# A gate on GpSimd's queue for batch 1's loads, in a fused FNet mixing and RWKV channel mix

## The chip, the cores and the metric

The kernel runs on one core of a Trainium2 chip. The core has five engines with a queue of instructions each: TensorE (PE, with its weight loads shown apart as PEld), VectorE (DVE), ScalarE (ACT), GpSimd (POOL) and SyncE (SP). They run independently of each other and meet at semaphores. Sixteen DMA engines move data between the main memory (DRAM) and the core's memory; here POOL issues all loads of x and of the weights, and SP nearly all stores of the output. The metric is the device time of one execution, in microseconds (us); lower is better.

## The reference

For each of 8 batches of x (3072 x 256), a two-dimensional Fourier transform of which the real part is kept, and then a channel mix with a shift by one row:

```python
X = np.fft.fft(x, axis=1)
X = np.fft.fft(X, axis=2)
x = X.real                                   # (8, 3072, 256)
x_prev = np.concatenate([zeros, x[:, :-1, :]], axis=1)
xk = mu_k * x + (1.0 - mu_k) * x_prev
xr = mu_r * x + (1.0 - mu_r) * x_prev
k = np.maximum(xk @ w_k, 0.0)                # 256 -> 1024
v = k * k @ w_v                              # 1024 -> 256
r = 1.0 / (1.0 + np.exp(-(xr @ w_r)))        # 256 -> 256
out = r * v
```

## The kernel before, in words

**One batch** passes through two halves. The transform uses the symmetry of a real input. Two copies of x are loaded for a batch, `xp` (rows in order) and `xm` (rows mirrored, fetched by a gather with a list of row numbers), each in two parts h = 0 and 1 (`load_xh`, L151). `fold` (L158) adds the two copies on DVE (L168 the bulk, L170 one column), `butterfly` (L173) splits the sum into an even and an odd part. Stage A (`a_sum`, `a_item`, `a_half`, L510 to 577) multiplies them with small tables on PE and leaves `a`; stage D (`d_units`, L579, with `d_evac` and `turned`, which repairs one column) goes on to `g_all`; stage C (`c_sums`, L624, or `c_pairs`, L651) gives the transform `y`. The results of PE lie in PSUM banks, and ACT or DVE copy them to the core's memory (L501 on DVE, L503 on ACT). `diff` and `mix` form xk and xr from y on DVE.

The channel mix runs over 48 chunks of 512 rows (8 batches, 2 mirrored halves m, 3 pieces). A chunk takes four steps of the main loop at the end of the kernel, some 2.2 us each. In a step PE multiplies with `w_k` (`k_products`, L738), ACT takes the positive part (L748), DVE or ACT squares it (L758, L756), PE multiplies an earlier chunk's squares with `w_v` (L779, L791 in the first chunks), and DVE multiplies the result with r and SP stores it (L801, L809). `r_item` (L760) gives r of a chunk: PE at L765 with `wr`, ACT at L770.

**The order of the work** is written out by hand. `at(step, f, ...)` and `event(step, ...)` put the transform of later batches between the chunks of earlier ones; `pin_order` at the end fixes the order on every engine to the order in which the code recorded it. Nothing else holds an instruction back than its semaphores: a load that is recorded at a late step starts as soon as POOL has done what stands ahead of it and the buffer is free. There are three buffers each for `xp` and `xm`, used in turn, and a load waits for the fold that read its buffer last.

**The start** is a stretch of its own. The tables are computed on the chip. Batch 0's x is loaded in six pieces (L242 to L249), and then `loads` (L441) puts on POOL's queue: the row numbers, the two halves of `w_k`, `w_v`, batch 1's first part (three loads: xp, one short xm, one long xm), the two halves of `w_r` for m = 0, and batch 1's second part (two loads). `loads_2`, recorded at step 4, follows with more row numbers and the weights for m = 1, and batch 2's loads after that. Meanwhile PE, DVE and ACT carry batch 0 through stages A, D and C in an order that mixes their pieces (L830 to L936). A few matmuls on zeros, `keep_busy` (L203), stand between them. The pieces around the change are, in the order of the code: two small pieces of stage D, one large piece with its first half evacuated by ACT (L854), one more piece of stage D (`w`), the first `c_sums` (slots 0 to 4), `turned(2, 4)` evacuated by DVE (L864), and the second half of the large piece evacuated by DVE (L865). Then come the first mixed columns (L869 on ACT, L874 on DVE), the `c_sums` of slots 5 to 8 and 9 to 16, and the first chunk's products.

Batch 1's first fold is on DVE at step 4 (`at(4, fold, 1, 0)`), its second at step 11; the first `r_item` is on PE at step 5. For later batches the loads of batch b + 3 are recorded 12 and 14 steps into batch b.

Of the kernel before, what the change touches and what calls it, by code (L numbers as in the profile page):

```python
# [11 lines left out]
INT32 = mybir.dt.int32  # L12
# [8 lines left out]
def _v(ap, extra_offset, free_dims):  # L21
    new_ap = [list(ap.ap[0])] + [[s, c] for (s, c) in free_dims]
    return dataclasses.replace(ap, offset=ap.offset + extra_offset, ap=new_ap)
# [16 lines left out]
def kernel(  # L40
# [20 lines left out]
    const = ctx.enter_context(tc.tile_pool(name="const", bufs=1))  # L61
# [44 lines left out]
    V = nc.vector  # L106
# [11 lines left out]
    def x_tiles(b, h):  # L118
        xp_t[b, h] = xp_sb[(2 * b + h - 1) % 3] if b or h else xp_00
        xm_t[b, h] = xm_sb[(2 * b + h) % 3]  # L120
# [6 lines left out]
    def load_p(b, h):  # L127
        r, n = 9 * h, 9 - h
        if b > 1:
            for g in range(2):  # L130
                src = dataclasses.replace(x[b, 32 * g + r:32 * g + r + 1, :],
                                          ap=[[64 * D, N1], [D, n], [1, D]])
                nc.gpsimd.dma_start(out=xp_t[b, h][64 * g:64 * g + N1, 0:n], in_=src)  # L133
            return
        src = dataclasses.replace(x[b, r:r + 1, :], ap=[[32 * D, 96], [D, n], [1, D]])
        nc.gpsimd.dma_start(out=xp_t[b, h][0:96, 0:n], in_=src)

    def gather(dst, src, idx):
        nc.gpsimd.indirect_dma_start(dst, None, src, bass.IndirectOffsetOnAxis(ap=idx, axis=0))  # L139

    def load_m(b, h, o, n, idx):
        gather(xm_t[b, h][0:parts(b), XM0 + o:XM0 + o + 256 * n],
               x.rearrange("b (s r) d -> (b s) (r d)", r=n), idx)

    def load_m0(b):
        if b == 0:
            gather(xm_00[:, 1:257], x.rearrange("b s d -> (b s) d"), idx_0[:, 0:1])
        else:
            load_m(b, 0, 2048, 1, (idx_g0 if b > 1 else idx_0)[:, b:b + 1])

    def load_xh(b, h):  # L151
        x_tiles(b, h)
        load_p(b, h)
        if h == 0:
            load_m0(b)
        load_m(b, h, 0, 8, (idx_g8 if b > 1 else idx_8)[:, b, h:h + 1])
# [74 lines left out]
    iota = nc.gpsimd.iota  # L231
# [191 lines left out]
    def rows():  # L423
        for a in range(2):
            for half in range(2):
                iota(_v(row_i[64 * half:64 * half + 64], a, [(3 - 2 * a, 2)]), pattern=[[0, 2]],
                     base=256 * a + half * (1 - 2 * a), channel_multiplier=2 - 4 * a)
        iota(row_i[0:1, 2:3], pattern=[[0, 1]], base=0, channel_multiplier=0)
        iota(_v(row_i[0:1], 1, [(2, 2)]), pattern=[[0, 2]], base=128, channel_multiplier=0)
# [11 lines left out]
    def loads():  # L441
        rows()
        for a in range(2):
            gather(wk_sb[0][a], moe_w_k, row_i[:, a:a + 1])
        nc.gpsimd.dma_start(out=wv_sb, in_=moe_w_v.rearrange("(fc p) v -> p fc v", p=128))
        load_xh(1, 0)
        for a in range(2):
            gather(wr_sb[0][a], moe_w_r, row_i[:, a:a + 1])
        load_xh(1, 1)

    def loads_2():
# [47 lines left out]
    def evac(out_ap, in_ap, eng):  # L499
        if eng == "V":  # L500
            V.tensor_copy(out=out_ap, in_=in_ap)  # L501
        else:
            nc.scalar.activation(out=out_ap, in_=in_ap, func=AF.Copy)  # L503
# [86 lines left out]
    def d_evac(ps, u0, n, bank, eng):  # L590
        evac(_v(g_all, 256 * u0, [(64, 2), (128, 2 * n), (1, 64)]),
             _v(ps, 0, [(bank, 2), (64, 2 * n), (1, 64)]), eng)
# [13 lines left out]
    def turned(u0, u1, ps=None, eng="A"):  # L606
        ps = ps_w() if ps is None else ps
        f128 = _v(g_all, 256 * u0 + 128, [(256, u1 - u0)])
        nc.tensor.matmul(out=ps[:, 0:u1 - u0], lhsT=turn, rhs=f128, start=True, stop=True)  # L609
        evac(f128, ps[:, 0:u1 - u0], eng)  # L610
# [222 lines left out]
    half_tables(mu_ps)  # L833
    V.tensor_copy(out=muf_t, in_=mu_ps[:, 0:6])
    loads()
    fold(0, 1, 0, 4)
    a_sum(0, 1, 0, "A")
# [25 lines left out]
    c_sums((first[:, 0:512], first[:, 512:1024]), 0, 5, 1)  # L863
    turned(2, 4, small[1][:, 256:258], "V")  # L864
    d_evac(fill[:, 256:1024], 4, 2, 512, "V")  # L865
    x_t[0, 0, 0] = mix_pool.tile([P, 2, 1536], FP16, name="x00")
    for a in range(2):
        t = x_t["t", a] = mix_pool.tile([P, 24, 64], FP16, name=f"t{a}")
# [28 lines left out]
    def at(step, f, *args):  # L897
        work.setdefault((step, "x" if f in (a_item, a_sum, d_item, d_small, c_item, c_tiles, turned, minus_0, r_item) else "w"),
                        []).append((f, args))
# [5 lines left out]
    def event(step, *items):  # L905
        work.setdefault((step, "e"), []).extend((f[0], f[1:]) for f in items)
        if len(items) > 2 and items[0][0] is not a_slots_0:
            early_v.add(step + 1)
# [102 lines left out]
    for b in range(B):  # L1011
        s0 = 24 * b

        for n, st0 in enumerate((2, 4, 6, 8) if b > 1 else ()):
            at(s0 + st0, mix, b, n // 2, 1, n % 2)
        if b and b + 3 < B:
            for h in range(2):
                at(s0 + 12 + 2 * h, load_xh, b + 3, h)
        t = b + 2
        if t < B:  # L1020
            if b:
                for n, st0 in enumerate((9, 10, 12, 14)):
                    at(s0 + st0, butterfly if n % 2 else fold, t, n // 2)
                for n, st0 in enumerate((27, 29, 31, 33)):
                    at(s0 + st0, d_item, t, n)
                at(s0 + 34, turned, 0, 13)
            c = [(c_pairs, t, 8 * n, (8, 8, 8, 4)[n], EV[n]) for n in range(4)]
            if t + 1 < B:
                event(s0 + ES[0], c[0], c[1], (a_half, t + 1, 0, 0, EV[4]))
                event(s0 + ES[1], c[2], c[3], (a_half, t + 1, 0, 1, EV[5]))  # L1030
                event(s0 + ES[2], (a_slots_0, t + 1), (a_half, t + 1, 1, 0, EV[6]), (a_half, t + 1, 1, 1, EV[7]))
            else:
                event(s0 + ES[0], *c[:2])
                event(s0 + ES[1], *c[2:])
        t = b + 1
        if b and t < B:
            at(s0 + 16, halves, t, 0, 15)
            at(s0 + 18, halves, t, 15, 27)
            for a in range(2):
                at(s0 + 19 + a, diff, t, 0, 26, (a,))  # L1040
                at(s0 + 21 + a, mix, t, 0, 0, a)
            at(s0 + 24, mix, t, 1, 0, 0)
            at(s0 + 25, mix, t, 1, 0, 1)
# [59 lines left out]
```

## Time and profile before

| | us |
|---|---|
| median of three runs | 441.21 (441.04 to 443.92) |
| the profiled execution, whole | 442.6 |
| its span, first to last instruction | 440.8 |
| PE busy in the span | 427.9 (97%) |
| DVE busy | 362.2 (82%) |
| ACT busy | 321.7 (73%) |
| POOL busy | 57.6 (13%) |

The profile is of one execution on the chip. The span lies inside the profiled time; 1.8 us are around it. All positions below are in microseconds from the start of the span. A row of the timeline gives the start, the duration, the engine, the line, the operation, what it writes and reads, the shape, how many instructions are merged, and in brackets how long the engine was idle before and what ended the wait; "remote" and "another core or an unknown queue" mean that the profile could not tell who ended it. A matmul's end is modelled. For a load, the row on POOL is only the issue; the data arrive later.

### The profile page before, as it was taken

What the parts mean: (1) busy time and instruction counts of PE and PEld (TensorE: products, weight loads), DVE (VectorE), ACT (ScalarE), POOL (GpSimd) and SP (SyncE); (2) the same over time, 40 slices, a digit from 0 to 9 for tenths busy, and PEclk for the clock granted to TensorE, in tenths of its full rate; (3) what the DMA queues carried; (4) which work ended last, traced back from release to release, by engine and by line L of the source; (5) the groups of instructions that cost most, each with busy time, mean ns of one, the idle gap of its engine ahead of it and who ended that gap; (6) DMA issues with size and microseconds to landing.
All of it is one profiled execution on the core that took longest, in us unless ns stands there. A gap on an engine that the chain in (4) does not pass through costs nothing.

```text
span 440.8 us, 9300 instructions
## 1 busy us (share of the span) xinstructions
PE 427.9 (97%) x3853; PEld 301.0 (68%) x3853; DVE 362.2 (82%) x554; ACT 321.7 (73%) x374; POOL 57.6 (13%) x83
## 2 busy tenths in 40 slices
PE   8699999999999999999999999999999999999995
PEld 3466766777777757677577776777776776766764
DVE  8589989998898968988699888989889857997553
ACT  7479898787877768687686778777777877666661
POOL 7862423004200120002100010000000000000000
PEclk9879999999999999999999999999999999999999
DMA  7999569239623493326732372322223223233334
GB/s 137 153 209 186 96 126 177 59 73 164 137 50 73 90 173 73 73 56 120 158 73 49 71 149 51 74 67 54 59 64 72 64 58 73 49 71 72 73 72 96
DMA packets 34990, 41.81 MB, mean 95 GB/s; under 512 B 4098, under 2 KB 31076, under 8 KB 34948
## 3 DMA queue, kind: packets, MB, share of 16 engines
q1 hardware_dynamic: 27524, 25.05, 24.2%
q0 software_dynamic: 7264, 16.04, 22.4%
q8 instruction: 30, 0.49, 0.5%
q10 hardware_dynamic: 160, 0.13, 0.1%
q14 instruction: 12, 0.10, 0.1%
HBM read 32.08 MB, written 25.17 MB: 130 GB/s over the span
## 4 chain that ended last, share of the span: by engine, by line
PE 94%; DVE 1%; DMA 1%; POOL 1%; issue 1%; another core or an unknown queue 0%; ACT 0%; POOLq 0%
PE psW L738 38%; PE psV L779 36%; PE psW L765 10%; PE psV L791 3%; PE psW L586 2%; PE psW L546 1%; PE psW L659 1%; DMA xm<-in_x_dram,idx 1%; PE psW L627 1%; POOL xm L139 1%; DVE pq L501 1%; PE psW L203 0%; PE psV L564 0%; PE psW L564 0%
## 5 line engine op out<-in xcount | busy, mean ns | idle before, releaser
L748 ACT ACTIVATE rl<-psW 128x1024 f16<-128x1024 f32 x192 | 195.6, 1025 | 91.4 <-PE psW L738 87.6
L738 PE MATMUL psW<-x,wk 128*128 128x512 f16 (+1 forms) x776 | 197.0, 380 | 0.8 <-DVE pq L501 0.7
L779 PE MATMUL psV<-wv_sb,k 128*128 128x256 f16 x1424 | 184.4, 273 | 0.2
L779 PEld LDWEIGHTS <-k 128*128 128x128 f16 x1424 | 136.9, 98 | 36.4 <-issue 0.7
L758 DVE TENSOR_TENSOR k<-rl 128x2048 f16<-128x2048 f16 (+1 forms) x101 | 116.3, 1152 | 32.9 <-ACT rl L748 32.5
L738 PEld LDWEIGHTS <-wk 128*128 128x128 f16 x776 | 75.6, 99 | 54.6 <-issue 2.2
L801 DVE SCALAR_TENSOR_TENSOR o<-psV,r 128x512 f32<-128x512 f32 (+1 forms) x97 | 65.8, 681 | 15.2 <-PE psV L779 13.5
L703 DVE TENSOR_TENSOR x<-y,t 128x1536 f16<-128x1536 f16 (+2 forms) x72 | 61.6, 861 | 2.1
L765 PE MATMUL psW<-wr,x 128*128 128x256 f16 x384 | 49.8, 273 | 0.0
L770 ACT ACTIVATE r<-psW 128x1024 f16<-128x1024 f32 x48 | 48.9, 1018 | 0.8 <-PE psW L765 0.8
L765 PEld LDWEIGHTS <-x 128*128 128x128 f16 x384 | 37.5, 98 | 14.3 <-issue 0.2
L133 POOL DMA_DIRECT2D xp<-in_x_dram x24 | 13.0, 546 | 187.5 <-DVE p L170 187.2
L503 ACT ACTIVATE a<-psW 128x832 f16<-128x832 f32 x31 | 26.1, 863 | 3.9 <-PE psW L546 1.4
L503 ACT ACTIVATE g_all<-psW 128x1024 f16<-128x1024 f32 (+5 forms) x36 | 25.3, 703 | 0.9 <-PE psW L609 0.6
L139 POOL DMA_INDIRECT xm<-in_x_dram,idx_g x18 | 23.6, 1311 | 5.7 <-issue 5.7
L168 DVE TENSOR_TENSOR p<-xp,xm 112x2304 f16<-112x2304 f16 (+5 forms) x19 | 21.0, 1105 | 0.8 <-DMA xm<-in_x_dram,idx 0.8
L692 DVE TENSOR_SCALAR t<-d,muf_t 128x1536 f16<-128x1536 f16 (+2 forms) x40 | 20.7, 527 | 0.0
L692 DVE TENSOR_SCALAR t<-d,mu_m 128x1536 f16<-128x1536 f16 x32 | 19.7, 614 | 0.0
L586 PEld LDWEIGHTS <-a 128*128 128x128 f16 x208 | 14.8, 102 | 6.7 <-issue 0.6
L503 ACT ACTIVATE pq<-psW 128x1024 f16<-128x1024 f32 (+1 forms) x18 | 15.2, 880 | 4.6 <-PE psW L659 4.6
L501 DVE CAST pq<-psW 128x1024 f16<-128x1024 f32 x6 | 7.3, 1225 | 13.0 <-PE psV L779 8.0
L179 DVE TENSOR_TENSOR eo<-p 112x1152 f16<-112x1152 f16 (+3 forms) x28 | 18.0, 683 | 0.0
(136 smaller groups left out, 215.8 us busy)
## 6 DMA issues: line engine op xcount, KB each, us to landing
out_dram<-o SPq DMA_DIRECT2D x190, 128.0 KB, 2.4
xp<-in_x_dram POOLq DMA_DIRECT2D x12, 216.0 KB
xp<-in_x_dram POOLq DMA_DIRECT2D x12, 192.0 KB
xp<-in_x_dram POOLq DMA_DIRECT2D x2, 432.0 KB
xp<-in_x_dram POOLq DMA_DIRECT2D x2, 384.0 KB
wv_sb<-in_moe_w_v_dram POOLq DMA_DIRECT2D x1, 512.0 KB
xm<-in_x_dram,idx_g POOLq DMA_INDIRECT x18
out_dram<-o ACTq DMA_DIRECT2D x2, 64.0 KB
```

What stands on the lines that cost most here:

```text
L139: nc.gpsimd.indirect_dma_start(dst, None, src, bass.IndirectOffsetOnAxis(ap=idx, axis=0))
L503: nc.scalar.activation(out=out_ap, in_=in_ap, func=AF.Copy)
L586: nc.tensor.matmul(out=ps[:, o:o + 128], lhsT=a_t[b][:, e, 2 * (u0 + i):2 * (u0 + i) + 2, :], rhs=w_eo[:, e], start=True, stop=True)
L692: V.tensor_scalar(out=dst, in0=src, scalar1=mu, scalar2=None, op0=ALU.mult)
L703: V.tensor_tensor(out=_v(x_t[b, j, m], o, [(64 * step, hi - lo), (step, 64)]), in0=y_t[b][:, lo + 3 * m:hi + 3 * m, a], in1=x_t["t", a][:, ...
L738: nc.tensor.matmul(out=st["k", ds][:, 512 * hs + lo:512 * hs + hi], lhsT=wk_sb[m][a][:, 128 * fc:128 * fc + 128], rhs=xk[:, a, 512 * i + l ...
L748: nc.scalar.activation(out=st["rl"][:, 2 * ds:2 * ds + 2], in_=st["k", ds].rearrange("p (f t) -> p f t", f=2), func=AF.Relu, bias=0.0, sca ...
L758: V.tensor_tensor(out=k2_t[c][:, lo:hi], in0=r, in1=r, op=ALU.mult)
L765: nc.tensor.matmul(out=ps[:, 256 * tb:256 * tb + 256], lhsT=x_t[b, 1, m][:, a, 512 * i + 128 * tb: 512 * i + 128 * tb + 128], rhs=wr_sb[m] ...
L770: nc.scalar.activation(out=st["r", c], in_=ps, func=AF.Sigmoid)
L779: nc.tensor.matmul(out=st["v", tb - h][:, 256 * h:256 * h + 256], lhsT=k2_t[c][:, fc, 128 * tb:128 * tb + 128], rhs=wv_sb[:, fc], start=(f ...
L801: V.scalar_tensor_tensor(out=o.rearrange("p a b -> p (a b)")[:, 0:256 * n], in0=st["v", t0][:, 0:256 * n], scalar=16.0, in1=st["r", c][:, ...
```

## The change

Batch 1's loads and the two loads of `w_r` for m = 0 leave `loads` and form a function of their own, `loads_1`. It begins with two new instructions on a new tile `gate` of one element: DVE writes it, and POOL writes it again, so that POOL's write waits for DVE's. In this group the two `w_r` gathers now come ahead of batch 1's loads. `loads_1` is recorded behind DVE's last evacuation of stage D in the start (L865 of the kernel before). `loads_2` and everything after it follow on POOL as before. The last hunk records the two loads of batch b + 3 at 4 and 22 steps into batch b in the place of 12 and 14.

```diff
         nc.gpsimd.dma_start(out=wv_sb, in_=moe_w_v.rearrange("(fc p) v -> p fc v", p=128))
-        load_xh(1, 0)
+
+
+    gate = const.tile([1, 1], INT32)
+
+    def loads_1():
+        V.memset(gate, 0)
+        iota(gate, pattern=[[0, 1]], base=0, channel_multiplier=0)
         for a in range(2):
             gather(wr_sb[0][a], moe_w_r, row_i[:, a:a + 1])
+        load_xh(1, 0)
         load_xh(1, 1)
...
     turned(2, 4, small[1][:, 256:258], "V")
     d_evac(fill[:, 256:1024], 4, 2, 512, "V")
+    loads_1()
     x_t[0, 0, 0] = mix_pool.tile([P, 2, 1536], FP16, name="x00")
...
             for h in range(2):
-                at(s0 + 12 + 2 * h, load_xh, b + 3, h)
+                at(s0 + 4 + 18 * h, load_xh, b + 3, h)
```

## The prediction

> **What bounds the kernel now.** I read the page's busy times first, then the chain of work that ended last, then the stretch of the chain around the change.
>
> ```profile
> PE 427.9 (97%) x3853; PEld 301.0 (68%) x3853; DVE 362.2 (82%) x554; ACT 321.7 (73%) x374; POOL 57.6 (13%) x83
> PEclk9879999999999999999999999999999999999999
> PE 94%; DVE 1%; DMA 1%; POOL 1%; issue 1%; another core or an unknown queue 0%; ACT 0%; POOLq 0%
> ```
>
> PE is the bound: 97% busy and 94% of the chain. What is lost or won in the start is therefore kept to the end, if PE receives it; an engine beside PE must first prove that it holds PE up. All 12.9 us in which PE is idle matter, and so does the third row: the granted clock is below full only in the first three of 40 slices. The chain in order of time has one piece in the start that no work fills:
>
> ```profile
> 7.98 5.35 DMA xm<-in_x_dram,idx
> ...
> 18.58 0.43 PE psV L609
> ...
> 19.04 0.17 DVE g_all L501
> ...
> 19.27 0.59 DVE g_all L501
> 19.86 2.08 another core or an unknown queue
> ...
> 21.97 0.18 DVE g_all L501
> ```
>
> For 2.08 us the chain stands at "an unknown queue". The timelines of DVE, ACT and PE there:
>
> ```profile
> 21.97 0.17 DVE L501 CAST g_all<-psV 128x2 f16<-128x2 f32 x1 [2.10 <-remote]
> 21.99 0.84 ACT L869 ACTIVATE t<-psW,mu_n 128x256 f16<-128x256 f32 x2 [3.00 <-remote]
> 19.60 0.18 PE L609 MATMUL psV<-g_all,turn 128*128 128x2 f16 x1
> 22.19 0.40 PE L627 MATMUL psW<-m_cs,g_all 64*128 64x128 f16 x4 [1.99 <-DVE g_all L501]
> ```
>
> DVE's cast of two columns needs only PE's `turned(2, 4)`, which began at 19.60 and is modelled 0.18 long. ACT needs the `c_sums` just ahead of it. Both engines go on within 0.02 us of each other at 21.97: PE's news of two finished pieces came some 2.1 us late. What else ran then is on POOL:
>
> ```profile
> 13.82 0.62 POOL L136 DMA_DIRECT2D xp<-in_x_dram  x1
> 14.73 0.97 POOL L139 DMA_INDIRECT xm<-in_x_dram,idx  x1 [0.30 <-issue]
> 16.01 0.93 POOL L139 DMA_INDIRECT xm<-in_x_dram,idx  x1 [0.30 <-issue]
> ...
> 18.50 0.94 POOL L139 DMA_INDIRECT wr<-in_moe_w_r_dram,row_i  x1 [0.30 <-issue]
> 19.44 0.60 POOL L136 DMA_DIRECT2D xp<-in_x_dram  x1
> 20.34 0.94 POOL L139 DMA_INDIRECT xm<-in_x_dram,idx  x1 [0.30 <-issue]
> ...
> 22.26 0.96 POOL L139 DMA_INDIRECT wk<-in_moe_w_k_dram,row_i  x1 [0.16 <-issue]
> 24.12 0.94 POOL L139 DMA_INDIRECT wk<-in_moe_w_k_dram,row_i  x1 [0.90 <-DMA xp<-in_x_dram]
> ```
>
> From 13.82 to 21.28 POOL issues exactly the loads that the change moves. The last of them, 20.34 to 21.28, lies in the wait. Elsewhere the same pattern of short, narrow matmuls under a gather looks alike (PE, then POOL):
>
> ```profile
> 106.30 0.64 PE L659 MATMUL psW<-m_cs,g_all 64*128 64x64 f16 x32
> 157.00 0.64 PE L659 MATMUL psW<-m_cs,g_all 64*128 64x64 f16 x32
> 158.56 0.21 PE L546 MATMUL psW<-w_h,eo 48*128 48x52 f16 x2 [0.51 <-issue]
> 209.59 0.64 PE L659 MATMUL psW<-m_cs,g_all 64*128 64x64 f16 x32
> 157.19 0.98 POOL L139 DMA_INDIRECT xm<-in_x_dram,idx_g  x1 [0.30 <-issue]
> ```
>
> At 157 a gather runs beside stage C, and PE stops for 0.51 with nothing to wait for; from this place to the same one a batch later takes 52.59, while the period before, 106.30 to 157.00, takes 50.70. So narrow matmuls and POOL's gathers seem to disturb each other, at a price between 0.5 and 2.1 each time. That is an inference from coinciding rows, no mechanism that a row names.
>
> **The change part by part.** *The new instructions.* DVE's write of one element falls between the cast of the next row and the column mix:
>
> ```profile
> 22.04 0.68 DVE L501 CAST g_all<-psW 128x512 f16<-128x512 f32 x1
> 22.87 1.13 DVE L874 SCALAR_TENSOR_TENSOR x<-psW,muf_t,t 128x128 f16<-128x128 f32 x4
> 21.97 0.12 POOL L457 IOTA idx_g<- 1x8 uint32 x1
> ```
>
> A write of one element should cost no more than the 0.17 of the two-column cast at 21.97, and DVE has a gap of 0.15 there (22.72 to 22.87): cost 0, or 0.17 without that cover. POOL's one-element write costs about 0.12 of POOL, and behind it everything on POOL waits: the two `w_r` gathers, batch 1's five loads, then the weights for m = 1 and batch 2.
>
> *The stall.* With the gate POOL issues nothing from 13.8 until DVE has passed L865, so no load is issued beside the two late pieces. If the coincidence is a cause, the 2.1 go: lower end 0 (another cause), upper end 2.5 (`turned(0, 2)` at 18.58 also stands under a gather and holds the chain 0.43, where the like piece at 19.60 is modelled 0.18). I take 2.1.
>
> *The clock.* The stages from here on, and the matmuls in them:
>
> ```profile
> 19.00:22.20 3.20, 0.74 (x12) 0.48 (x12) 1.06 (x5) 0.21 (x1) 2.66 (x8) 0.86 1.20 206
> 22.20:28.10 5.90, 5.90 (x47) 4.28 (x48) 5.33 (x14) 3.63 (x10) 4.33 (x5) 0.50 1.11 209
> 28.10:33.10 5.00, 4.98 (x46) 2.92 (x45) 4.29 (x11) 4.89 (x8) 3.14 (x4) 1.00 1.14 209
> 33.10:45.00 11.90, 11.90 (x90) 8.25 (x88) 11.60 (x29) 11.23 (x13) 2.43 (x3) 1.00 0.87 173
> 24.25 1.89 PE L738 MATMUL psW<-x,wk 128*128 128x256 f16 x8
> 28.42 1.89 PE L738 MATMUL psW<-x,wk 128*128 128x512 f16 x8
> ```
>
> (Columns of the first four: stretch, length, busy time of PE, PEld, DVE, ACT, POOL, granted clock, DMA share, GB/s.) PE works 0.74 of 3.20 us around the stall, and directly behind it the granted clock is 0.50 for 5.90 us: eight products of 256 columns take as long as eight of 512 later. Without the stall the clock may stay up. PE itself would win more than 1.5, but DVE is busy 5.33 of 5.90 and 4.29 of 5.00, and each chunk needs its squares: the gain is between 0 and DVE's idle 0.57 + 0.71 = 1.28. I take 0.6, as the clock may still drop at some point of the start.
>
> *New neighbours.* The queue that starts at 20.6 (22.72 less 2.1) puts the `w_r` gathers at 21.05 to 23.3, beside `turned(4, 8)` and the `c_sums` of slots 9 to 16; in the kernel before these lay between two gathers (22.26 to 23.22 and from 24.12). Price between 0 and 2.1; I take the 0.5 of the one-gather case at 158.56.
>
> *The deadline.* What could be late is batch 1's first fold:
>
> ```profile
> 33.05 1.35 DVE L168 TENSOR_TENSOR p<-xp,xm 96x2304 f16<-96x2304 f16 x1
> xp<-in_x_dram POOLq DMA_DIRECT2D x2, 432.0 KB
> xp<-in_x_dram POOLq DMA_DIRECT2D x2, 384.0 KB
> ```
>
> From 20.6 POOL needs 0.15, two gathers at 1.25, 0.62, 1.27 and 1.23: the long xm is issued by 26.4. Its 384 KB (the size of the second row's xp) at the stage's 209 GB/s take 1.9, so 28.3 at the earliest; at the latest 5.35 after its issue began at 25.5, as the chain's first row shows for a load with a backlog: 30.8. The fold moves to 33.05 - 2.1 - 0.6 = 30.35. So it finds its data between 2.0 early and 0.5 late; I take 0, as DMA has run dry before the gate. If this cover goes, DVE (11.60 of 11.90 busy in 33.10 to 45.00) passes nearly all lateness on. The `w_r` gathers come first, for PE at step 5, and the other loads have more than 10 us.
>
> The Trainium skill speaks against the change here: in "DMA: Bandwidth & Descriptors", Rules for kernel authors, a DMA under compute is to be issued early and waited for late. By that rule the 9 us of delay are only risk; the trace agrees that an early load costs no wait on its data, but not that it is free.
>
> *The last hunk.* In the built program of the changed kernel the order on POOL of all loads of batches 2 to 7 is unchanged, and each waits for the same fold as before. POOL does not know the steps: cost 0.
>
> The sum: 2.1 + 0.6 - 0.5 = 2.2 less. The profiled execution would take 442.6 - 2.2 = 440.4. It stood 1.4 above the median, so the median comes to 441.2 - 2.2 = **439.0**.
>
> **The rivals.** *The stall stays.* Its cause would lie in PE or its instruction supply, and the gate opens at 22.7; the fold's data land by 32.9 at the latest, against 33.05. Against it: both engines are released together with POOL's gather just over. For it: many gathers run beside wide matmuls unharmed. Time: 441.2, of 440.8 to 442. The Trainium skill supports it: "SBUF — State Buffer", Who interferes with whom, holds that a DMA never contends with a compute engine. By that rule the forecast's 2.1 would not exist; the row at 158.56 speaks against it, though no row names the port.
>
> *More goes.* The clock stays up, the new neighbours cost nothing: 441.2 - 2.5 - 1.28 = 437.4. If the shifted loads also miss stage C at 157 and 209, twice 52.59 - 50.70 = 1.9 more: 433.6. Against it: the loads there start from the same folds.
>
> *Slower: the stall moves and multiplies.* Two more narrow pieces of stage C follow:
>
> ```profile
> 32.20 0.62 PE L627 MATMUL psW<-m_cs,g_all 64*128 64x128 f16 x16
> 35.47 0.29 PE L627 MATMUL psW<-m_cs,g_all 64*128 64x128 f16 x4
> ```
>
> Behind the gate POOL has a queue without a pause that reaches them and slots 9 to 16, now all at the full clock. At 2.1 each, two give 441.2 - 2.1 + 4.2 = 443.3, three 445.4, and a late fold on top 445.9. It decides from the second hit on; POOL's row at 24.12 beside PE's untouched row at 24.25 speaks against it.
>
> *The gate holds nothing.* POOL's order is its program, and its write of the tile waits for DVE's: as good as excluded.
>
> **How the numbers follow.** Forecast 0.42, the stall stays 0.20, more goes 0.20, slower 0.18. A change of 1% (4.4 us) is about what a measurement of this kernel can tell from no change. Faster by more: 0.14 of "more goes" and 0.02 of the forecast. Slower by more: 0.12 of the last rival, 0.02 of the second. The range, 435.8 to 443.6, leaves out the far half of "more goes" and of "slower".
>
> **What would show it.** Right: POOL empty from 13.8 to about 20.6, no "remote" wait near 20, the granted clock above 0.50 behind it, DVE's first fold of batch 1 with no wait for a DMA, and everything behind 60 shifted by one amount. Wrong: the 2.1 stand at the same `turned(2, 4)`; a wait of the fold for xm; new idle time of PE at L627 behind the gate; or stage C at 106 disturbed as at 157.

## The result, and the profile after

The changed kernel takes **439.04 us** (median of 18 runs, 437.24 to 442.74). The kernel before, run beside it, takes 441.99 (18 runs, 441.04 to 444.29). The ratio is 0.9932 with an interval of 0.9912 to 0.9952: 2.95 us less. That is clear of the noise, but under the 1% (4.4 us) that the prediction took as the least that can be told from no change. Profiled: 438.3 us with a span of 436.5, against 442.6 and 440.8.

The page of the kernel after has the same bound, and a clock that stays up in all 40 slices:

```profile
PE 424.1 (97%) x3853; PEld 298.5 (68%) x3853; DVE 361.9 (83%) x555; ACT 321.8 (74%) x374; POOL 59.9 (14%) x84
PEclk9999999999999999999999999999999999999999
```

The chain of the kernel after through the same stretch (start, duration, what):

```profile
17.29 0.17 DVE g_all L508
...
17.52 0.61 DVE g_all L508
18.13 0.04 issue
```

The 2.08 us at "an unknown queue" are gone: 0.04 us stand in their place. The timeline of DVE, then that of POOL:

```profile
18.06 0.17 DVE L508 CAST g_all<-psV 128x2 f16<-128x2 f32 x1
...
18.76 0.06 DVE L451 MEMSET gate<- 1x1 int32 x1
...
20.48 0.69 DVE L508 CAST y<-psV 128x512 f16<-128x512 f32 x1 [0.47 <-PE psV L634]
...
28.77 1.35 DVE L168 TENSOR_TENSOR p<-xp,xm 96x2304 f16<-96x2304 f16 x1 [0.19 <-issue]
...
53.10 0.69 DVE L808 SCALAR_TENSOR_TENSOR o<-psV,r 128x512 f32<-128x512 f32 x1 [0.92 <-DMA out_dram<-o]
```

```profile
18.92 0.12 POOL L452 IOTA gate<- 1x1 int32 x1 [4.97 <-DVE gate L451]
19.21 0.99 POOL L139 DMA_INDIRECT wr<-in_moe_w_r_dram,row_i  x1 [0.16 <-issue]
```

The cast of `turned(2, 4)` at 18.06 waits for nothing (before: 2.10). POOL is idle for 4.97 us and then issues behind the gate. A smaller wait is new: DVE's cast of y stands 0.47 for PE's `c_sums` (L634), while POOL issues a gather of `w_r`. The first fold of batch 1 begins at 28.77 and waits for no DMA. PE in the kernel after, at the first products and at stage C:

```profile
19.65 1.34 PE L745 MATMUL psW<-x,wk 128*128 128x256 f16 x8
...
101.82 0.64 PE L666 MATMUL psW<-m_cs,g_all 64*128 64x64 f16 x32
...
152.53 0.64 PE L666 MATMUL psW<-m_cs,g_all 64*128 64x64 f16 x32
...
154.28 0.23 PE L553 MATMUL psW<-w_h,eo 48*128 48x52 f16 x2 [0.74 <-issue]
...
205.32 0.64 PE L666 MATMUL psW<-m_cs,g_all 64*128 64x64 f16 x32
```

The first products come 4.60 us sooner (24.25 before), stage C 4.48 (106.30), 4.47 (157.00) and 4.27 (209.59), and the end 4.3. So all of it is won in the start, and 0.2 of it is lost again behind the second stage C, where the pause is still there, 0.74 where it was 0.51.

Of the 4.60, the clock of these two executions gave a good part. The cast of `turned(0, 2)` already comes 1.75 sooner, 17.29 against 19.04. The only difference ahead of it in the program is that POOL no longer issues the loads of batch 1 and of `w_r` from 13.8 on. In the kernel before the granted clock was half there (windows of the kernel before, then after; columns as in the prediction):

```profile
16.00:18.00 2.00, 2.00 (x13) 1.13 (x12) 1.11 (x3) 0.34 (x1) 1.69 (x2) 0.53 1.10 131
```

```profile
16.00:18.00 2.00, 1.81 (x29) 1.48 (x29) 1.56 (x7) 0.98 (x2) 0.00 (x0) 1.00 1.09 140
```

The clock does not explain all of the 1.75. The matmul of `turned(0, 2)` began 1.35 sooner (PE before, then after):

```profile
18.42 0.17 PE L609 MATMUL psV<-g_all,turn 128*128 128x2 f16 x1
```

```profile
17.07 0.18 PE L616 MATMUL psV<-g_all,turn 128*128 128x2 f16 x1
```

From there to DVE's cast it took 0.62 before, at the full clock, and 0.22 after. So this piece too was told late, by 0.40. From its cast to the cast of `turned(2, 4)` it is 0.77 us and not 2.93. That difference, 2.16, is the stall that the prediction named.

### The profile page after: what moved, and what is told of

Read it like the earlier page. It is cut to its first block, busy times and chain, and to the rows that moved or that the text cites. A ratio compares the mean times of both kernels' runs of the same rounds, so it can differ in the third digit from the quotient of the medians.

```text
span 436.5 us, 9300 instructions
## 1 busy us (share of the span) xinstructions
PE 424.1 (97%) x3853; PEld 298.5 (68%) x3853; DVE 361.9 (83%) x555; ACT 321.8 (74%) x374; POOL 59.9 (14%) x84
## 4 chain that ended last, share of the span: by engine, by line
PE 87%; DVE 6%; DMA 3%; issue 1%; POOL 1%; ACT 1%; DVEq 0%; POOLq 0%; SPq 0%
PE psV L786 36%; PE psW L745 35%; PE psW L772 9%; DMA out_dram<-o 2%; PE psW L593 2%; PE psW L553 2%; PE psW L666 1%; DMA xm<-in_x_dram,idx 1%; DVE x L710 1%; DVE k L765 1%; POOL xm L139 1%; DVE t L699 1%; DVE o L808 1%; PE psW L634 0%; DVE p L168 0%
## 5 line engine op out<-in xcount | busy, mean ns | idle before, releaser
L699 DVE TENSOR_SCALAR t<-d,muf_t 128x1536 f16<-128x1536 f16 (+2 forms) x40 | 20.6, 526 | 0.0
L510 ACT ACTIVATE pq<-psW 128x1024 f16<-128x1024 f32 (+1 forms) x18 | 15.2, 880 | 4.8 <-PE psW L666 4.8
```

Of the source, the lines that this page charges most:

```text
L699: V.tensor_scalar(out=dst, in0=src, scalar1=mu, scalar2=None, op0=ALU.mult)
```

## The experiments

Three theories on the stall. **A**: POOL's issuing of loads beside PE's narrow matmuls makes PE's news late (the prediction's inference). **B**: it is the amount of data in flight. **C**: it is PE's own, or chance, and the change only moved it. The kernels ran in groups on three chips, each beside the kernel before, which took 441.16 us (31 runs), 441.75 (23) and 435.23 (35) there. The third chip turned out to matter. Which chip the first comparison used is not recorded; its 441.99 is like the first two.

### More gathers ahead of the gate (first chip)

```diff
+        spare = const.tile([P, 4, 256], FP16)
+        for n in range(4):
+            gather(spare[:, n], moe_w_r, row_i[:, 0:1])
```

Four small gathers into a tile that nobody reads are put at the end of `loads`, so that POOL issues from 14.0 to 18.9 again.

> The changed kernel with four more small gathers of w_r rows (64 KB each, into a spare tile that nothing reads) on POOL between the load of w_v and the gate, so that POOL issues gathers from about 14.3 to 19.2 as it did before the change, but with little data. Theory A (it is POOL's issuing beside the narrow matmuls of stages D and C that delays the news of finished matmuls): the casts of turned(0, 2) and turned(2, 4) on DVE wait again, 0.5 to 2 us in sum, the gate opens 0.5 to 2 us later than at 18.8, and the time is 0.5 to 2 us over the changed kernel's 439.0. Theory B (it is the amount of data in flight): no new wait, the gate opens at 18.8 to 19.3, the time is 439.0 within 0.5. Theory C (it was PE's own, such as its instruction supply at that place, or chance): the same as B.

Measured: 440.57 us (10 runs), ratio 0.9981 (0.9961 to 1.0001). DVE's timeline:

```profile
18.24 0.17 DVE L511 CAST g_all<-psV 128x2 f16<-128x2 f32 x1 [0.86 <-PE psV L619]
...
19.76 0.17 DVE L511 CAST g_all<-psV 128x2 f16<-128x2 f32 x1 [0.69 <-PE psV L619]
```

Both two-column casts wait again, 0.86 and 0.69, and most of the gain is gone. The gathers' data are small (64 KB each), so this speaks for A. One thing does not fit its words: the issue of the last spare gather ended at 18.92 (17.98 and 0.94), POOL then stood idle, and the news still came only at 19.76. What delays it outlasts the issue.

### More data, no issue by POOL (first chip)

```diff
+    spare = const.tile([P, 3, 1024], FP32)
+    def traffic():
...
+        for n in range(3):
+            nc.sync.dma_start(out=spare[:, n], in_=x[5:6].rearrange(
+                "b (p s) d -> p (b s d)", p=128)[:, 1024 * n:1024 * n + 1024])
...
+    traffic()
```

SP loads 1.5 MB into a spare tile, started at 15.2 behind a small write of DVE; POOL stays idle behind its gate.

> The changed kernel with 1.5 MB of x loaded by SP into a spare tile that nothing reads, started at about 14.7 behind a write of DVE, so that the DMA engines are as full from 15 to 20 as before the change, while POOL stays idle. Theory A: no wait of the casts near 17 to 18, the gate opens at about 18.9; the time may be up to 1 us over 439.0 if batch 1's loads queue behind the traffic and the first fold waits. Theory B: the casts of turned(0, 2) and turned(2, 4) wait again by 1 to 2 us, and the time is 441 or more. Theory C: as A.

Measured: 440.73 us (10 runs), 0.9982 (0.9956 to 1.0007). The casts of the two-column pieces don't wait, but the first fold does:

```profile
18.57 0.17 DVE L515 CAST g_all<-psV 128x2 f16<-128x2 f32 x1
```

```profile
30.73 1.36 DVE L168 TENSOR_TENSOR p<-xp,xm 96x2304 f16<-96x2304 f16 x1 [1.59 <-DMA xm<-in_x_dram,idx]
```

At the two-column pieces this tests little, as few of the spare bytes had moved by then (from 17 to 18 the DMA engines moved 142 GB/s, 154 in the kernel after). Behind them it tests more. From 19 to 21 they moved four times what they moved in the kernel after (the windows of this run, then of the kernel after), and the `c_sums` of slots 9 to 16, which ran then, were told without a wait (DVE's cast of y):

```profile
19.00:21.00 2.00, 1.87 (x29) 1.26 (x26) 1.94 (x7) 1.30 (x5) 1.11 (x2) 1.00 1.18 309
```

```profile
19.00:21.00 2.00, 1.86 (x26) 1.21 (x25) 1.53 (x5) 1.42 (x4) 1.53 (x3) 1.00 0.52 73
```

```profile
20.43 0.68 DVE L515 CAST y<-psV 128x512 f16<-128x512 f32 x1
```

So theory B falls. But a gather of `w_r`, issued from 19.72 to 20.71, stood beside the same `c_sums`: a gather does not delay every narrow piece beside it. The time is lost elsewhere: the spare data delay batch 1's x, and DVE waits 1.59. That is the price of the prediction's deadline, met by other means.

### The gate later (first chip)

```diff
     def loads_1():
         V.memset(gate, 0)
         iota(gate, pattern=[[0, 1]], base=0, channel_multiplier=0)
+        load_xh(1, 0)
         for a in range(2):
             gather(wr_sb[0][a], moe_w_r, row_i[:, a:a + 1])
-        load_xh(1, 0)
...
-    loads_1()
...
     y_evac(0, 5, 4, w)
+    loads_1()
```

> The changed kernel with the gate moved on, behind DVE's copy of y from the sums of slots 9 to 16 (it ran at 20.48 to 21.17), and with batch 1's first part ahead of the w_r gathers, so that its long xm is issued at about the same time as before (23.4 to 24.3 against 23.6 to 24.5). Theory A: the sums of slots 9 to 16 are told on time, DVE's copy of y starts 0.7 to 1.0 earlier and the time is 0.3 to 1.0 under the changed kernel, unless the fold, which found its data with 0.1 to spare, gives it back. Theories B and C: DVE's copy of y starts where it did, at 20.5, and the time is that of the changed kernel or up to 1 us more, as the weights and the second part come later.

Measured: 440.4 us (12 runs), 0.997 (0.995 to 0.9991). DVE's cast of y has no wait left, so the collision of the new neighbours is gone. But `w_r` comes too late, and so does batch 1's x, as theory A had allowed (DVE, then PE):

```profile
23.39 0.68 DVE L508 CAST y<-psV 128x512 f16<-128x512 f32 x1
...
24.02 0.06 DVE L451 MEMSET gate<- 1x1 int32 x1
...
32.46 1.36 DVE L168 TENSOR_TENSOR p<-xp,xm 96x2304 f16<-96x2304 f16 x1 [1.21 <-DMA xm<-in_x_dram,idx]
```

```profile
33.91 0.92 PE L772 MATMUL psW<-wr,x 128*128 128x256 f16 x7 [0.82 <-DMA wr<-in_moe_w_r_dram,row_i]
```

The window for the gate is narrow: opened at 24.02, with x ahead of `w_r`, it holds up the first fold by 1.21 and the first `r_item` by 0.82.

### The gate sooner (second chip)

```diff
     c_tiles(0)
+    loads_1()
     turned(0, 2, small[0][:, 256:258], "V")
...
-    loads_1()
```

> After with the gate five DVE instructions sooner, ahead of the cast of the first two-column piece: it opens near 17.1, and the two w_r gathers are issued at 17.4 to 19.6, beside both two-column pieces and the first c_sums, 1.7 us sooner than in after. Theory A: the cast of turned(2, 4) waits 0.5 to 2.1 once more, everything behind it is later by as much, the fold's data come 1.7 earlier than needed: 439.5 to 441.0. Theory C (the stall of before was PE's own, or went with the number of loads in flight): as after, 438.7 to 439.2.

Measured: 443.47 us (10 runs), 1.003 (1.0012 to 1.0047): slower than the kernel before. But the expected place is wrong. A gather was issued from 18.49 to 19.48, beside both two-column pieces; yet the cast of `turned(2, 4)` waits for nothing, and the wait of the cast ahead of it stands in a stretch of half clock, where its matmul began only at 18.63 (DVE's timeline, then the windows):

```profile
18.91 0.17 DVE L508 CAST g_all<-psV 128x2 f16<-128x2 f32 x1 [0.78 <-PE psV L616]
...
48.11 0.69 DVE L808 SCALAR_TENSOR_TENSOR o<-psV,r 128x512 f32<-128x512 f32 x1 [4.10 <-DMA out_dram<-o]
```

```profile
16.00:18.00 2.00, 2.00 (x14) 1.33 (x13) 1.18 (x4) 0.45 (x2) 0.00 (x0) 0.50 1.12 147
```

The late news comes one piece further on, behind the second gather (19.79 to 20.73): ACT's copy of `turned(4, 8)`, whose matmul began at 20.57, waits 0.86, where in the kernel after it waits 0.23.

```profile
21.33 0.19 ACT L510 ACTIVATE g_all<-psW 128x4 f16<-128x4 f32 x1 [0.86 <-PE psW L616]
```

So theory A's price is there, but not at each narrow piece beside a gather.

The large item is the second row of DVE: it stands 4.10 us for an output buffer, and PE with it. The DMA view of the stretch from 33 to 46 has the stores:

```profile
out_dram<-o SPq DMA_DIRECT2D x6, 128.0 KB, 10.3
```

A store (the last figure is the median to its landing) takes 10.3 us behind a burst of loads. The same view of the kernel before, over the same stretch:

```profile
out_dram<-o SPq DMA_DIRECT2D x4, 128.0 KB, 4.5
```

The kernel after pays a little of it too: at 53.10 its DVE waits 0.92 for an output buffer. So the position of the gate seems to set the phase between the first stores and the loads of batch 2 as well. No theory had this. Slow stores alone do not make the 4.10: in the run with more gathers they take 10.7 in the same stretch, and DVE waits 1.08.

### Batch 1's first part ahead of the weights (second chip)

```diff
         iota(gate, pattern=[[0, 1]], base=0, channel_multiplier=0)
+        load_xh(1, 0)
         for a in range(2):
             gather(wr_sb[0][a], moe_w_r, row_i[:, a:a + 1])
-        load_xh(1, 0)
         load_xh(1, 1)
```

> After with batch 1's first part issued ahead of the two w_r gathers, at the same gate. A plain load then stands first behind the gate, 19.1 to 19.7, and the first gather begins near 20.0 and not at 19.2. Theory A, if the gather at 19.2 to 20.2 is what makes the wait of 0.47 at DVE's cast of y (20.48): that wait shrinks to under 0.2 or moves to the next piece, the first fold finds its data 2 us earlier, and the time is 438.2 to 439.0; if a plain load disturbs as much as a gather, the wait stays at 0.4 to 0.6 and the time is 439.0. In neither case does the first r_item wait for w_r, which is issued by 24.5 (in the later gate it waited when they were issued at 28.4 to 32). Theory C: the wait stays as it is, 439.0.

Measured: 438.06 us (5 runs), 0.9913 (0.9887 to 0.994). In its profile the cast of y begins at 21.02 with no wait, as A expected. The time lies just under what was expected, and against after (0.9932) the intervals overlap, so this order is not shown to be faster. A plain load was issued from 20.24 to 20.81 beside the `c_sums` that this cast waits for (20.07 to 20.81), and did not delay them. But one gather in the run with more data did not either.

### Plain loads in the place of the gathers (second chip)

```diff
+        spare = const.tile([P, 8, 256], FP16)
+        for n in range(8):
+            nc.gpsimd.dma_start(out=spare[:, n], in_=moe_w_r[0:128, :])
```

> After with eight plain loads of the same weights on POOL's queue ahead of the gate, in the place of the four gathers of the first experiment, so that POOL issues without pause from 14 to about 18.8, through the narrow pieces of stage D. If any issue of a load by POOL delays PE's news, DVE's casts of the two-column pieces at 17.3 and 18.1 wait 0.5 to 1 each again, as with the gathers (0.86 and 0.69), and the time is 440.0 to 441.0. If it is the gathers alone (they write descriptors from a list of row numbers), the casts wait under 0.2 as in after and the time is 438.7 to 439.5.

Measured: 444.86 us (10 runs), 1.0056 (1.003 to 1.0082). It answers another question than the one asked (POOL, then DVE):

```profile
17.87 0.64 POOL L448 DMA_DIRECT2D spare<-in_moe_w_r_dram  x1 [0.76 <-DMA wk<-in_moe_w_k_dram,row_i]
22.40 0.53 POOL L448 DMA_DIRECT2D spare<-in_moe_w_r_dram  x1 [3.90 <-DMA wv_sb<-in_moe_w_v_dram]
```

```profile
34.04 1.36 DVE L168 TENSOR_TENSOR p<-xp,xm 96x2304 f16<-96x2304 f16 x1 [3.56 <-DMA xm<-in_x_dram,idx]
```

With so many loads on its queue POOL waits until an older load has landed, 3.90 us, and the gate's write stands behind it. Batch 1's x is late, and the fold waits 3.56. No issue stood beside the two-column pieces, so the question stayed open.

### Gates in the main loop (first chip, then second)

The prediction's second evidence was stage C at 157 and 209, under gathers that the change does not move. The first of these two kernels gates the load of (b + 3, 0) alone, the second both loads:

```diff
+    gate_2 = const.tile([1, 1], INT32)
+    def gated_load(b, h):
+        V.memset(gate_2, 0)
+        iota(gate_2, pattern=[[0, 1]], base=0, channel_multiplier=0)
+        load_xh(b, h)
...
-            for h in range(2):
-                at(s0 + 4 + 18 * h, load_xh, b + 3, h)
+            at(s0 + 13, gated_load, b + 3, 0)
+            at(s0 + 22, gated_load, b + 3, 1)
```

> The changed kernel with one more gate for each of the batches 4 to 7: the loads of batch b + 3 wait for a write of DVE that is recorded 13 steps into batch b, behind the first narrow matmuls of stage C (which ran at 101.8, 152.5 and 205.3). Theory A: the pauses of PE in stage C at 153 and 206 go, each of the two long periods of 52.6 comes down to 50.7, and the time is 3 to 4 us under the changed kernel (about 435.5); the pause at 66 may go too, 0.5 to 1 more. Theories B and C: the loads only move, other places are disturbed in their stead or the pauses stay, and the time is 439.0 within 1.

> After with both loads of batch b + 3 gated in the main loop: the first behind a DVE write at step 13, the second behind one at step 22 (the run before gated only the first, measured 438.9, lost the pauses at 153 and 206, and got new ones of 0.2 to 0.3 at 114.5, 165.6, 216.8 and 268 where the second load followed in the same burst). Theory A (POOL issuing gathers beside stage C's narrow matmuls makes PE's news late): with the second load moved out of all three events the new pauses of 0.2 to 0.3 go too; each period of the loop is 0.3 to 0.5 shorter, three or four periods, so 437.2 to 438.2. Theory C (the pauses are PE's own and only move about): pauses of the same sum appear at other places, 438.6 to 439.2.

Measured: with one gate 438.89 us (8 runs), 0.9944 (0.9919 to 0.9968); with both **436.09** (6 runs), 0.9867 (0.9836 to 0.9898). With one gate the time is what theories B and C expected (439.0 within 1), not A's 435.5. The profile shows both sides: the pauses at 153 and 206 go, but each of the four periods from 104.11 to 308.75 takes 51.1 to 51.2, as one pause comes up at the next event, under the second load (ACT, then PE):

```profile
113.67 1.51 ACT L517 ACTIVATE pq<-psW 128x1024 f16<-128x1024 f32 x2 [0.60 <-PE psW L560]
```

```profile
114.74 1.89 PE L752 MATMUL psW<-x,wk 128*128 128x512 f16 x8 [0.23 <-ACT pq L517]
```

With both gates that is gone as well, and the gain is larger than expected (437.2 to 438.2, worked out from the kernel after and the first chip). Stage C in this kernel:

```profile
152.21 0.64 PE L673 MATMUL psW<-m_cs,g_all 64*128 64x64 f16 x32
...
202.92 0.64 PE L673 MATMUL psW<-m_cs,g_all 64*128 64x64 f16 x32
...
253.62 0.64 PE L673 MATMUL psW<-m_cs,g_all 64*128 64x64 f16 x32
```

The periods are 50.71 and 50.70, exactly the undisturbed 50.70 of the prediction; the kernel after needs 52.79 from 152.53 to 205.32. On these chips the pause follows POOL's issue from place to place and goes with it: A holds in this, and C in its form of a fixed place falls.

### The third chip

This is the kernel before with the last hunk alone; its built program has the same instructions in the same order on every engine as the kernel before, so it also gives a profile of that program on this chip.

```diff
-                at(s0 + 12 + 2 * h, load_xh, b + 3, h)
+                at(s0 + 4 + 18 * h, load_xh, b + 3, h)
```

> The kernel before with the last hunk alone (steps 4 and 22 in the place of 12 and 14). Its built program has the same instructions in the same order on every engine as the kernel before, so the prediction's cost of 0 for this hunk says a ratio of 1.000 within 0.2%, 441 to 442.5. Its single executions also show how the time of this program hangs on the granted clock: if the clock term of the prediction was a price that the stall itself caused, all of them have a mean clock near 0.988, as the profile of before; if it is a chance of the execution, some have 0.998 and more, and these take 439 to 440.5.

Measured: 435.38 us (12 runs), 1.0017 (0.9999 to 1.0034): the hunk costs nothing, as predicted. But the level, expected at 441 to 442.5, is 6.5 us below the second chip's. Whether the stall causes the clock's drops could not be seen, as this chip has no stall; two of the 12 runs have a mean clock of 0.999, the others 0.987 to 0.996. In its profile, DVE, POOL, PE and ACT in this order:

```profile
16.89 0.17 DVE L501 CAST g_all<-psV 128x2 f16<-128x2 f32 x1 [0.18 <-PE psV L609]
```

```profile
16.36 0.93 POOL L139 DMA_INDIRECT xm<-in_x_dram,idx  x1 [0.31 <-issue]
...
151.60 0.98 POOL L139 DMA_INDIRECT xm<-in_x_dram,idx_g  x1 [0.30 <-issue]
```

```profile
151.42 0.64 PE L659 MATMUL psW<-m_cs,g_all 64*128 64x64 f16 x32
151.90 0.37 PE L546 MATMUL psW<-w_h,eo 48*128 48x52 f16 x16
...
202.12 0.64 PE L659 MATMUL psW<-m_cs,g_all 64*128 64x64 f16 x32
```

```profile
151.87 1.02 ACT L503 ACTIVATE pq<-psW 128x1024 f16<-128x1024 f32 x1 [0.20 <-PE psW L659]
```

Gathers lie beside the narrow pieces as in the profile before: one is issued from 16.36 to 17.29, over the `turned(0, 2)` that begins at 16.67 and is cast at 16.89, and one 0.18 behind the start of stage C (before: 157.19 against 157.00). Yet nothing waits longer than 0.2 there. PE's sixteen L546 matmuls run in one group, where before they broke off for 0.51, and the period to the next stage C is 50.70. ACT hears of stage C 0.45 after it began; in the profile before it is 1.58:

```profile
158.58 1.02 ACT L503 ACTIVATE pq<-psW 128x1024 f16<-128x1024 f32 x1 [1.32 <-PE psW L659]
```

The row of the waits by engine and line (us in total, times, longest) for the kernel before; after; after with both loop gates, second chip; and the program of before on the third chip:

```profile
ACT pq L503 <- PE psW L659: 4.6, 12, 1.3
```

```profile
ACT pq L510 <- PE psW L666: 4.8, 12, 1.5
```

```profile
ACT pq L517 <- PE psW L673: 2.3, 12, 0.2
```

```profile
ACT pq L503 <- PE psW L659: 2.3, 12, 0.2
```

Two loop gates on the second chip and no gate at all on the third give the same 2.3. So where there is a pause, on the first two chips, it comes and goes with the gathers beside narrow matmuls. They are not enough for it: two pieces beside a gather were told on time there (in the run with more data and with the gate sooner), and on the third chip stage C is never late.

How a gather holds up PE is open. "Late news" is itself a reading: at stage C PE breaks off within sixteen equal matmuls with nothing to wait for (0.51 in the kernel before, 0.74 in the kernel after), so PE itself may be late. Its instruction supply, which the prediction named as a rival, was not tested as the way by which a gather acts.

Three more kernels ran on this chip, to tell A from C, to combine, and to try plain loads again; here there was no stall to move, and the first and the last miss what every theory expected.

```diff
+    gate_2 = const.tile([1, 1], INT32)
...
-            for h in range(2):
-                at(s0 + 12 + 2 * h, load_xh, b + 3, h)
+            at(s0 + 13, gated_load, b + 3, 0)
+            at(s0 + 22, gated_load, b + 3, 1)
```

> The kernel before with the two gates in the main loop alone (the first load of batch b + 3 behind a DVE write at step 13, the second at step 22), and nothing changed in the start. Theory A: the start keeps its stall of 2.1 and the loop gains what it gained on top of after (439.04 to 436.09, 2.95): 438.3 to 439.3, and the two places add up. Theory C (both changes only shift the phase of the same pauses): the gains don't add up, and this alone gives 436 to 437.5 or nothing, 441 to 442.

Measured: the kernel before with the two loop gates alone takes 435.18 us (12 runs), 1.0007 (0.9982 to 1.0031). Whether the two gains add up where the stall exists was not tested.

```diff
         iota(gate, pattern=[[0, 1]], base=0, channel_multiplier=0)
+        load_xh(1, 0)
         for a in range(2):
             gather(wr_sb[0][a], moe_w_r, row_i[:, a:a + 1])
-        load_xh(1, 0)
...
-                at(s0 + 4 + 18 * h, load_xh, b + 3, h)
+            at(s0 + 13, gated_load, b + 3, 0)
+            at(s0 + 22, gated_load, b + 3, 1)
```

> After with both loop gates and with batch 1's first part ahead of the two w_r gathers: the two changes that were faster each, together. If they are independent: 436.09 less 0 to 1.0, so 435.1 to 436.1. The cast of y behind the gate waits under 0.2 and the first fold of batch 1 finds its data. If the order behind the gate is worth nothing by itself, 436.1; if the earlier x makes the burst of loads collide with the first output stores, 437 to 441, with DVE waiting for an output buffer.

Measured: after with both loop gates and the x first takes 435.02 us (12 runs), 0.9992 (0.9972 to 1.0012): as fast as the kernel before on this chip, and inside the expected numbers, but not for the expected reason.

```diff
+    def early_loads():
+        V.memset(gate, 0)
+        iota(gate, pattern=[[0, 1]], base=0, channel_multiplier=0)
+        for n in range(4):
+            nc.gpsimd.dma_start(out=spare[:, n], in_=moe_w_r[0:128, :])
...
         d_units(0, ps, u, 1, 128)
+        if u:
+            early_loads()
         d_evac(ps, u, 1, 128, "AV"[u])
```

> After with four plain loads of weights into a spare tile on POOL's queue behind a gate of their own, which DVE opens ahead of its cast at 16.6, so that POOL issues plain loads from about 16.4 to 18.9, beside the narrow two-column pieces (17.1 to 18.1), and with only seven loads on its queue (the run with eight plain loads had POOL wait for a landed load, so no issue stood beside the pieces). If any issue by POOL makes PE's news late, the casts of the two-column pieces at 17.3 and 18.1 wait 0.5 to 1 each as with the four gathers, 440.0 to 441.0. If only gathers do, they wait under 0.2, 438.7 to 439.7.

Measured: 436.29 us (10 runs), 1.0033 (1.0012 to 1.0054). POOL issues the four plain loads where it was wanted, and no cast waits; but gathers make none wait here either, so plain loads against gathers stays open. What costs 1.06 us is the fold (POOL, then DVE):

```profile
16.66 2.16 POOL L464 DMA_DIRECT2D spare<-in_moe_w_r_dram  x4
```

```profile
29.65 1.36 DVE L168 TENSOR_TENSOR p<-xp,xm 96x2304 f16<-96x2304 f16 x1 [1.83 <-DMA xm<-in_x_dram,idx]
```

The gate opened when it did in the kernel after (POOL's write at 18.96, there 18.92), but DVE reaches the fold 0.8 sooner, and the x behind the spare loads lands later than 28.77, where the fold began there. The changed kernel itself did not run on this chip, so what it takes there was not measured.

## Why the prediction was right, and where it was not

The forecast of 439.0 met 439.04. Part of that is luck of the baseline: the three runs it started from had a median of 441.21, and 18 runs give 441.99. The forecast gain was 2.2, the measured one is 2.95. The mechanism, issues of POOL that hold up narrow pieces of PE in the start, was right as far as the runs of the first two chips show it; how it works stays open.

- *The new instructions, 0.* Right: DVE's write takes 0.06 in the gap ahead of the column mix (18.76, next row of DVE at 18.88).
- *The stall, 2.1.* Right in size for `turned(2, 4)`, 2.16, and all of it went. `turned(0, 2)` gave another 0.40, which the prediction had only in its upper end. (That end, 2.5, adds the whole 0.43 of the chain; less the 0.18 that the piece takes by itself it would be 2.3.) The inference from coinciding rows stood the test on the two chips on which it could be tested, though not at every piece. The Trainium skill's rule against it ("SBUF — State Buffer", Who interferes with whom: a DMA never contends with a compute engine) would have left the stall in place. On those chips ACT's waits for stage C fall from 4.8 to 2.3 us when only POOL's loads are moved, so as a forecast of what loads cost PE the rule failed there; whether the ports of that memory have a part in it, no run shows. The third chip's 2.3 without any gate agrees with it. What the inference lacked is that the disturbance depends on the chip, so the gain does too.
- *The clock, 0.6.* The right direction, sized somewhat low. (The row with the clock is the second of the prediction's first fence, not the third.) In 54 runs of the kernel before on the first two chips the mean granted clock was never above 0.996; of the 18 runs after, nine had 0.997 or more, with a median of 438.28, and nine less, with 440.11. Runs without a drop are 1.8 faster, and half of the runs are such: an estimate of 0.9. That the stall brings the drops is likely from these counts, but not shown: on the third chip, without a stall, 22 of 35 runs have a mean clock of 0.996 or less too. The bound of 1.28 set by DVE's idle time was wrong as a bound on one run, because the clock drops at various places of the start, ahead of the stall too.
- *New neighbours, 0.5.* Right in this profile: 0.47 at DVE's cast of y, beside a `w_r` gather. With the gate behind that cast, or x first, the wait is gone. That the size was met is luck: in the run with more data the same gather lay beside the same `c_sums`, and nothing waited.
- *The deadline, 0.* Right, but thin: the gate opened at 18.92 and not at 20.6, the fold began at 28.77 and not at 30.35, 0.19 behind DVE's instruction ahead of it and without a DMA wait. With 1.5 MB more in flight it waited 1.59, with four more small loads 1.83, with the gate at 24.02 1.21.
- *The last hunk, 0.* Right: 1.0017 (0.9999 to 1.0034), measured on the third chip.
- Not in the list of steps: the first stores against the shifted burst of loads, 0.92 of DVE in after and 4.10 with the gate sooner. Of the signs of being right one came in part only: the shift behind 60 is not one amount (4.48, 4.47, 4.27).

The terms as measured give 2.16 + 0.40 + 0.9 - 0.5 = 3.0, beside the 2.95. The stall's part is from one profile each and the clock's an estimate, so that they meet so closely is in part chance. Of the rivals, "the stall stays" and "slower" did not come. "More goes" named 1.9 us twice at stage C: that gain is real, and needed gates of its own.

The kernel with two more gates in the loop beats the kernel before on the second chip, 436.09 against 441.75. Its ratio of 0.9867 (0.9836 to 0.9898) lies below the 0.9932 (0.9912 to 0.9952) of the kernel after, but the two were not measured side by side. On the third chip its variant with x first costs nothing, 435.02 against 435.23.

## What to carry to other kernels

Where two engines are released together and late for no reason that a row names, look at what POOL issues in that stretch, and move the issue under wide matmuls with a gate of one element; the place must be tried: opened five DVE instructions sooner, the kernel was slower than before the change (443.47 against 441.75), and some 5 us later, with x first, over half of the gain was gone (0.997 against 0.9932). Run such a gain on a second and a third chip before relying on it: here one chip had nothing to win. When loads are moved, check the stores that share the DMA engines with them, and how many buffers wait for those stores.

## What the runs showed of the hardware

The same program takes 441.75 us on one chip and 435.23 on another, at like clocks (runs with a mean granted clock of 0.990 to 0.992 have medians of 441.5 and 436.0). Most of the difference goes when POOL's gathers are moved away from narrow matmuls: with the gates in the start and in the loop the second chip comes to 436.09. Why the third chip is free of it, no trace here shows.

Where there were pauses, the late pieces were told 0.4 to 0.8 us after a gather's issue had ended, and not at its end: in the kernel before at 19.04, 21.97 and 158.56 (issues ended at 18.20, 21.28 and 158.17), with more gathers at 18.24 and 19.76 (17.67 and 18.92), and PE itself went on at 154.28 and 155.73 in the kernel after (153.70 and 154.95). The smaller wait at the cast of y in the kernel after ended 0.28 behind one. In these profiles a gather's issue takes POOL mostly 0.9 to 1.0 us, a plain load of x about 0.6.

The granted clock drops to one half in stretches of 3.4 us or twice that (14.46 to 17.87 and 21.3 to 28.1 in the profile before, by its clock records; 15.6 to 19.0 with the gate sooner, and again from 49.7 to 53.1 behind the wait for the output buffer; none in the profile after), at a place that differs between executions. Executions of after with and without such a drop have medians 1.8 us apart. The Trainium skill ("TensorE: Matmul & The Clock Gate", Part 1) gives the same 3.4 us as the window in which the activity of PE is watched; the traces agree.

A store of 128 KB that SP issues between 33 and 46 us lands in 4.5 us (median) in the kernel before, and in 10.3 behind the burst of loads with the gate sooner.
